# Moving V through TensorE 512 columns at a time, in four column groups and register-addressed loops, in a one-token attention-and-MLP kernel

## The chip, the cores and the metric

One core of one Trainium2 chip. The metric is device time in microseconds (us). The spans of the profile are 1.4 to 1.9 us shorter than the time of the same run, because they run from the first to the last instruction of the program. Executions of the kernel before agree within 0.3%.

## The reference, cut to what matters

One token, two branches, and a scalar gate that mixes them. Branch A is grouped-query attention over the last 4096 positions of a cache, with 32 query heads and 16 key/value heads of size 128. Branch B is an MLP with GELU.

```python
W = min(4096, max(256, Sk // 4))                     # 4096
q = (x @ wq)                                          # 576 -> 32 heads x 128
k = repeat(k_cache[:, :, Sk - W:, :], 2);  v = the same of v_cache
p = softmax(q k^T * Dh**-0.5);  o = p v
a = o.reshape(4096) @ wo                              # 4096 -> 576
b = gelu(x @ w1 + b1) @ w2 + b2                       # 576 -> 4608 -> 576
return g * a + (1 - g) * b                            # g = sigmoid(sum(x * gate_w))
```

All inputs are bf16. The kernel must read K and V (16.8 MB each) and four weight matrices: 53.6 MB in all, for very little arithmetic.

## The kernel before

All large loads are issued in one queue, in program order: w1, wq, eight pieces of K, half of w2, V in groups of four heads (groups 0 to 2 as one load each, group 3 as two halves), wo in two halves, and the rest of w2 in three pieces. The buffers are shared. Their tags are A to D, and a load waits until the last reader of its buffer has finished. V group 3 goes into the buffer of V group 0 (tag C), and wo into that of V group 1 (tag D).

In the V stage each 128x128 block of V is the stationary operand, and 8 columns of probabilities move through it. That is 512 pairs of a weight load and a tiny matmul.

```python
p_t = kt_pool.tile([P, NCK, 8, HB], BF16, name="p_t", tag="kt")
pt = kt_pool.tile([P, NCK, Hq], BF16, name="pt", tag="kt")
# ... exp into p_t, transpose into pt ...
o_ps = ps_m.tile([P, Hq, 1], FP32, name="o_ps", tag="m")
for g in range(NG):                                   # NG = 4 groups of 4 heads
    v_t = big.tile([P, NCK, Dh], BF16, name="v_t", tag="CDAC"[g])
    src = ...
    for u in range(2 if g == NG - 1 else 1):
        n = NCK // 2 if g == NG - 1 else NCK
        nc.sync.dma_start(out=v_t[:, u * n : (u + 1) * n, :]..., in_=src[...])
    for c in range(NCK):                              # NCK = 128
        nc.tensor.matmul(o_ps[:, 8 * g : 8 * g + 8, 0], lhsT=v_t[:, c, :],
                         rhs=pt[:, c, 8 * g : 8 * g + 8],
                         start=(c == 0), stop=(c == NCK - 1))
wo_t = big.tile([P, RO, D], BF16, name="wo_t", tag="D")
# ... load wo in two halves, the rest of w2 in three pieces ...
# ... om = o_ps * (gate / softmax sum), ov = its heads regrouped ...
for r in range(RO):                                   # 32 rows of wo, two matmuls each
    y_add(ov[:, r : r + 1], wo_t[:, r, :])
for f in range(NJ, NF):                               # second half of w2
    y_add(gt[:, f : f + 1], w2_t[:, f, :], stop=(f == NF - 1))
# ... output row, store ...
```

## Time and profile before

| | before |
|---|---|
| time | 134.61 us (134.55 to 134.67, 2 runs) |
| span of the profile | 133.3 us |
| bytes moved | 53.78 MB, mean 403 GB/s |

The profile page cuts the span into 40 slices of 3.33 us each. A digit is the busy share in tenths, and PEclk is the clock granted to TensorE in tenths.

```profile
PE   0239995066499769769779450008923951445881
PEclk9999999999999999999999995555555555558679
DMA  5999989899999999999999999999999999999950
```

The DMA row is 9 from the second slice almost to the end. TensorE (PE) has idle slices, and its clock stands at half in the last third, yet nothing follows from that: the kernel is one uninterrupted stream of loads. The timeline of PE in the last third shows the same. Its columns are start, length, then engine, line and operation; in brackets is the idle time before, and what ended it.

```profile
90.98 6.04 PE L387 MATMUL o_ps<-pt,v_t 128*128 128x8 bf16 x220
99.66 1.10 PE L387 MATMUL o_ps<-pt,v_t 128*128 128x8 bf16 x36 [2.65 <-issue]
102.98 3.71 PE L387 MATMUL o_ps<-pt,v_t 128*128 128x8 bf16 x128 [2.22 <-DMA v_t<-in_A_v_cache_dram]
107.88 1.87 PE L387 MATMUL o_ps<-pt,v_t 128*128 128x8 bf16 x64 [1.19 <-DMA v_t<-in_A_v_cache_dram]
112.79 1.87 PE L387 MATMUL o_ps<-pt,v_t 128*128 128x8 bf16 x64 [3.04 <-DMA v_t<-in_A_v_cache_dram]
118.29 3.52 PE L178 MATMUL y_ps<-wo_t,ov 128*1 128x288 bf16 x32 [3.04 <-DMA wo_t<-in_A_wo_dram]
129.40 1.14 PE L178 MATMUL y_ps<-w_t,gt 128*1 128x288 bf16 x16 [0.40 <-DMA w_t<-in_B_w_dram]
```

A V group of 128 pairs takes 3.7 us (103.0 to 106.7). From the third group on, PE then waits for the next landing. The 64 matmuls with wo run while later loads are in flight, so only the last 16 with w2 are exposed at the end. The DMA issues in the same timeline show how early the queue is refilled. Each line is the first issue of a line of the kernel, and its length runs to the last issue.

```profile
62.22 33.56 SPq L382 DMA_DIRECT2D v_t<-in_A_v_cache_dram  x5
100.79 0.81 SPq L400 DMA_DIRECT2D wo_t<-in_A_wo_dram  x2
101.66 1.37 SPq L402 DMA_DIRECT2D w_t<-in_B_w_dram  x3
```

The last load is issued near 103 us and lands near 130 us, so at that point 27 us of transfers are queued. So the V stage should be able to run somewhat slower at no cost, as long as buffers come free in time to keep that queue filled.

### The profile page before, as it was taken

The numbers are of one execution on the slowest core, as the hardware profiler recorded it, in microseconds if no ns is written. First come the engines' busy times: TensorE is split into PE (matmuls) and PEld (weight loads), VectorE is DVE, ScalarE is ACT, GpSimd is POOL, SyncE is SP. The second block draws the span as 40 slices with busy tenths as digits, with TensorE's granted clock in tenths as the row PEclk, the third lists the DMA queues.
The fourth block names the chain that finished last, engine by engine and source line by source line (L and its number), as shares of the span: only waits on it lengthen the run. The fifth ranks groups of instructions, "written<-read, shape, count | busy, mean of one in ns | idle before, by whom it ended". The sixth has DMA issues, their size and how long they took to land.

```text
span 133.3 us, 2458 instructions
## 1 busy us (share of the span) xinstructions
PE 78.1 (59%) x1126; PEld 51.4 (39%) x1126; DVE 55.2 (41%) x80; ACT 13.0 (10%) x25; POOL 0.7 (1%) x6
## 2 busy tenths in 40 slices
PE   0239995066499769769779450008923951445881
PEld 0118995065134323223233230008913951423540
DVE  6177002202988988988984710663000000100001
ACT  3000000003000000000000059930000000000001
POOL 2000000000000000000000000000000000000000
PEclk9999999999999999999999995555555555558679
DMA  5999989899999999999999999999999999999950
GB/s 155 400 461 436 488 359 487 360 428 428 428 418 428 438 413 420 428 433 428 455 417 441 457 413 403 452 462 403 413 438 403 413 433 427 436 420 399 414 205 0
DMA packets 3190, 53.78 MB, mean 403 GB/s; under 512 B 358, under 2 KB 362, under 8 KB 620
## 3 DMA queue, kind: packets, MB, share of 16 engines
q1 hardware_dynamic: 3170, 53.61, 95.0%
q8 instruction: 9, 0.15, 0.4%
q10 hardware_dynamic: 10, 0.01, 0.0%
q14 instruction: 1, 0.01, 0.0%
HBM read 53.62 MB, written 0.00 MB: 402 GB/s over the span
## 4 chain that ended last, share of the span: by engine, by line
DMA 66%; PE 12%; DVE 8%; ACT 7%; issue 3%; SPq 2%; DVEq 0%
DMA k_t<-in_A_k_cache_dram 26%; DMA w_t<-in_B_w_dram 20%; DMA wq_t<-in_A_wq_dram 20%; ACT p_t L336 7%; PE o_ps L387 5%; DVE kt L285 3%; PE q_ps L242 3%; DVE pt L344 2%; DVE m L306 2%; PE s_ps L294 1%; PE y_ps L178 1%; SPq L77 1%; SPq L400 1%; PE t_ps L362 0%; DVE out_row L422 0%
## 5 line engine op out<-in xcount | busy, mean ns | idle before, releaser
L285 DVE STREAM_TRANSPOSE kt<-k_t 128x2048 f32<-128x2048 f32 x16 | 36.0, 2290 | 11.4 <-DMA k_t<-in_A_k_cache_dram 11.4
L294 PE MATMUL s_ps<-kt,qz_flat 128*128 128x512 bf16 x128 | 31.9, 396 | 9.3 <-DVE kt L285 9.3
L294 PEld LDWEIGHTS <-qz_flat 128*128 128x128 bf16 x128 | 12.8, 100 | 28.1 <-issue 14.3
L387 PE MATMUL o_ps<-pt,v_t 128*128 128x8 bf16 x512 | 14.6, 168 | 9.1 <-DMA v_t<-in_A_v_cache_dram 6.5
L387 PEld LDWEIGHTS <-v_t 128*128 128x128 bf16 x512 | 14.3, 105 | 9.5 <-DMA v_t<-in_A_v_cache_dram 6.7
L336 ACT ACTIVATE p_t<-s_ps,negm 128x512 bf16<-128x512 f32 x8 | 9.7, 1411 | 44.7 <-DVE negm L327 44.7
L204 PE MATMUL h_ps<-x,w_t 128*128 128x2 bf16 x162 | 10.2, 202 | 0.0
L204 PEld LDWEIGHTS <-w_t 128*128 128x128 bf16 x162 | 10.1, 163 | 0.0
L178 PE MATMUL y_ps<-wo_t,ov 128*1 128x288 bf16 x64 | 6.8, 393 | 5.0 <-DMA wo_t<-in_A_wo_dram 5.0
L405 DVE TENSOR_TENSOR om<-o_ps,rgh 128x128 bf16<-128x128 f32 x1 | 0.3, 292 | 22.8 <-PE o_ps L387 22.8
L344 DVE STREAM_TRANSPOSE pt<-p_t 128x2048 bf16<-128x2048 bf16 x2 | 4.6, 2311 | 7.4 <-ACT p_t L336 7.4
L362 PE MATMUL t_ps<-ls,ones 128*128 128x32 f32 x2 | 0.6, 396 | 11.9 <-DVE ls L360 11.9
L242 PE MATMUL q_ps<-x,wq_t 128*128 128x2 bf16 x144 | 4.0, 166 | 5.9 <-DMA wq_t<-in_A_wq_dram 5.9
L422 DVE CAST out_row<-y_ps 1x288 bf16<-1x288 f32 x1 | 0.4, 445 | 15.1 <-PE y_ps L178 15.1
L178 PEld LDWEIGHTS <-ov 128*1 128x1 bf16 x64 | 3.7, 110 | 7.7 <-issue 4.9
L178 PE MATMUL y_ps<-w_t,gt 128*1 128x288 bf16 x72 | 5.9, 298 | 0.6 <-DMA w_t<-in_B_w_dram 0.6
L242 PEld LDWEIGHTS <-wq_t 128*128 128x128 bf16 x144 | 3.9, 104 | 6.0 <-DMA wq_t<-in_A_wq_dram 6.0
L362 PEld LDWEIGHTS t_ps<-ls,ones 128*128 128x128 f32 x2 | 0.5, 310 | 12.2 <-issue 12.2
L421 ACT CAST out_row<-y_ps 1x288 bf16<-1x288 f32 x1 | 0.4, 390 | 42.9 <-PE y_ps L178 42.9
L178 PEld LDWEIGHTS <-gt 128*1 128x1 bf16 x72 | 3.4, 86 | 2.8 <-issue 1.5
L213 DVE COPY hacc<-h_ps 128x36 f32<-128x36 f32 x1 | 0.2, 196 | 9.4 <-PE h_ps L204 9.4
L306 DVE TENSOR_REDUCE m<-s_ps 128x2 f32<-128x2048 f32 x1 | 2.3, 2290 | 2.0 <-PE s_ps L294 2.0
(68 smaller groups left out, 26.9 us busy)
## 6 DMA issues: line engine op xcount, KB each, us to landing
k_t<-in_A_k_cache_dram SPq DMA_DIRECT2D x8, 2048.0 KB, 32.0
v_t<-in_A_v_cache_dram SPq DMA_DIRECT2D x3, 4096.0 KB, 29.8
wq_t<-in_A_wq_dram SPq DMA_DIRECT2D x1, 4608.0 KB, 26.1
wo_t<-in_A_wo_dram SPq DMA_DIRECT2D x2, 2304.0 KB, 20.0
v_t<-in_A_v_cache_dram SPq DMA_DIRECT2D x2, 2048.0 KB
w_t<-in_B_w_dram SPq DMA_DIRECT2D x1, 2880.0 KB, 14.7
w_t<-in_B_w_dram SPq DMA_DIRECT2D x1, 2592.0 KB, 11.3
w_t<-in_B_w_dram SPq DMA_DIRECT2D x1, 2304.0 KB, 8.3
```

The lines of the kernel that those rows point to most:

```text
L77: nc.sync.dma_start(out=w1_t[:, i0:i1, :], in_=w1_src[:, i0:i1, :])
L178: nc.tensor.matmul(y_out[s], lhsT=vec, rhs=row[:, s * DH : (s + 1) * DH], start=start, stop=stop, skip_group_check=True,)
L204: nc.tensor.matmul(h_ps[:, j:NF:NJ], lhsT=w1_t[:, i, j:FH:NJ], rhs=x2[:, i, :], start=False, stop=(i == NI - 1 and j == NJ - 1), skip_grou ...
L242: nc.tensor.matmul(q_ps[:, j : Hq : Hq // 2], lhsT=wq_t[:, i, j * Dh : (j + 1) * Dh], rhs=x2[:, i, :], start=(i == 0 and j == 0), stop=(i ...
L285: nc.vector.transpose(out=kt[:, u * half : (u + 1) * half].bitcast(FP32), in_=k_t[:, f, u * SL // 2 : (u + 1) * SL // 2, :] .rearrange("p ...
L294: nc.tensor.matmul(s_ps[:, u * 512 : (u + 1) * 512].rearrange("p (c k) -> p c k", k=32), lhsT=qz[:, h0 // 2, j, :], rhs=kv[:, u * SL // 4 ...
L306: nc.vector.reduce_max(out=m2[:], in_=s_ps[:].rearrange("p (n b) -> p b n", b=2), axis=AX.X)
L336: nc.scalar.activation(out=p_t[:, cs, :, b], in_=s_ps[:].rearrange("p (c k u b) -> p u b c k", k=8, u=2, b=2)[:, f, b % 2], func=ACT.Exp, ...
L344: nc.vector.transpose(out=pt[:, cs, :].rearrange("p c h -> p (c h)"), in_=p_t[:, cs, :, :].rearrange("p c k b -> p (c k b)"),)
L362: nc.tensor.matmul(t_ps[:], lhsT=ones[:], rhs=ls[:], start=True, stop=True)
L387: nc.tensor.matmul(o_ps[:, 8 * g : 8 * g + 8, 0], lhsT=v_t[:, c, :], rhs=pt[:, c, 8 * g : 8 * g + 8], start=(c == 0), stop=(c == NCK - 1),)
L400: nc.sync.dma_start(out=wo_t[:, r0:r1, :], in_=wo_src[:, r0:r1, :])
```

## The change

The intent is to issue fewer PE instructions. V becomes the moving operand, 512 columns (four blocks) at a time. The stationary operand is 32 columns of probabilities (4 blocks x 8 heads), loaded into one of four column groups of the array. Of each 32 x 512 product only the four diagonal blocks are wanted, so VectorE (DVE) masks and adds them, and an fp32 matmul with a selector sums the rest. The 128 matmuls stand in loops on PE with register addresses (the place of each operand is computed by PE's sequencer, the part of PE that issues its instructions, from the loop counter). Each loop is inside a critical section of the scheduler: a stretch that waits at its entry as a whole. The diff, cut:

```diff
+def grouped_matmul(nc, out, lhsT, rhs, col):
+    pe = nc.tensor
+    return pe.add_instruction(
+        mybir.InstMatmult(
+            start_tensor_calc=False, stop_tensor_calc=False,
+            tile_size=(128, 32), tile_position=(0, 32 * col), ...
-    pt = kt_pool.tile([P, NCK, Hq], BF16, name="pt", tag="kt")
+    pt = kt_pool.tile([P, NG, NCK, 8], BF16, name="pt", tag="kt")
...
+    # m4: four masks; zb: zeros; o4: four PSUM banks, zeroed by four matmuls
+    o_part = const.tile([P, NG, Dh], FP32, name="o_part")
...
-        for c in range(NCK):
-            nc.tensor.matmul(o_ps[:, 8 * g : 8 * g + 8, 0], lhsT=v_t[:, c, :], ...)
+            with tc.tile_critical():
+                with nc.tensor.Fori(u * n // 16, (u + 1) * n // 16) as it:
+                    for j in range(4):
+                        grouped_matmul(
+                            nc,
+                            o4[32 * j : 32 * j + 32, g, :, :].rearrange("p c d -> p (c d)"),
+                            pt[:, g, :, :].rearrange("p c h -> p (c h)")[
+                                :, bass.ds((it * 16 + 4 * j) * 8, 32)
+                            ],
+                            vf[:, bass.ds((it * 16 + 4 * j) * Dh, 4 * Dh)],
+                            j,
+                        )
+        nc.vector.tensor_scalar(out=o_part[:, g, :], in0=o4[:, g, 0, :], scalar1=m4[:, 0:1], ...)
+        for c in range(1, 4):
+            nc.vector.scalar_tensor_tensor(out=o_part[:, g, :], in0=o4[:, g, c, :], ...)
+        nc.tensor.matmul(o_ps[:, 8 * g : 8 * g + 8, 0], lhsT=o_part[:, g, :], rhs=lo8[:], start=True, stop=True)
```

What the diff does not show is what the scheduler makes of the critical sections. I read this from the order of instructions, and the semaphores they wait for, in the built program:

| loop | may start when (besides its own V) | what waits for its end |
|---|---|---|
| V0 | V1 has landed | load of V3, first half |
| V1 | V2 has landed | load of wo, first half |
| V2 | V3, first half, has landed | |
| V3, first half (3a) | wo, first half, has landed | load of V3, second half, and behind it wo's second half and the rest of w2 |
| V3, second half (3b) | wo, second half, has landed | the output |

More of the change, by code (lines that the diff above doesn't have):

```diff
@@ L13 @@
 AX = mybir.AxisListType
+def grouped_matmul(nc, out, lhsT, rhs, col):
+    pe = nc.tensor
+    return pe.add_instruction(
+        mybir.InstMatmult(
+            start_tensor_calc=False,
+            stop_tensor_calc=False,
+            tile_size=(128, 32),
+            tile_position=(0, 32 * col),
+            bass_skip_group_check=True,
+            name=nc.get_next_instruction_name(),
+            engine=mybir.EngineType.PE,
+            ins=[pe.lower_ap(rhs), pe.lower_ap(lhsT, for_matmul_weights=True)],
+            outs=[pe.lower_ap(out)],
+        )
+    )
 @with_exitstack
@@ L344 @@
         nc.vector.transpose(
-            out=pt[:, cs, :].rearrange("p c h -> p (c h)"),
-            in_=p_t[:, cs, :, :].rearrange("p c k b -> p (c k b)"),
+            out=pt[:, :, cs, :].rearrange("p g c h -> p c g h"),
+            in_=p_t[:, cs, :, :].rearrange("p c (g k) b -> p c g (k b)", g=NG),
         )
@@ L371 @@
     )
+    m4 = const.tile([P, 4], FP32, name="m4")
+    nc.vector.reduce_sum(out=m4[:], in_=lo32[:].rearrange("p (c h) -> p c h", c=4), axis=AX.X)
+    zb = const.tile([P, P], BF16, name="zb")
+    nc.vector.memset(zb[:].bitcast(FP32), 0.0)
     o_ps = ps_m.tile([P, Hq, 1], FP32, name="o_ps", tag="m")
+    o4 = ps_s.tile([P, NG, 4, Dh], FP32, name="o4", tag="s_ps")
+    o_part = const.tile([P, NG, Dh], FP32, name="o_part")
+    for g in range(NG):
+        nc.tensor.matmul(
+            o4[:, g, :, :].rearrange("p c d -> p (c d)"),
+            lhsT=zb[:],
+            rhs=zb[:, 0:1].to_broadcast([P, 4 * Dh]),
+            start=True,
+            stop=False,
+            skip_group_check=True,
+        )
     for g in range(NG):
@@ L379 @@
         )
+        vf = v_t[:].rearrange("p c d -> p (c d)")
         for u in range(2 if g == NG - 1 else 1):
@@ L385 @@
             )
-        for c in range(NCK):
-            nc.tensor.matmul(
-                o_ps[:, 8 * g : 8 * g + 8, 0],
-                lhsT=v_t[:, c, :],
-                rhs=pt[:, c, 8 * g : 8 * g + 8],
-                start=(c == 0),
-                stop=(c == NCK - 1),
-            )
+            with tc.tile_critical():
[9 more added lines that the diff above has]
+                            j,
+                        )
+        nc.vector.tensor_scalar(
+            out=o_part[:, g, :], in0=o4[:, g, 0, :], scalar1=m4[:, 0:1], scalar2=None, op0=ALU.mult
+        )
+        for c in range(1, 4):
+            nc.vector.scalar_tensor_tensor(
+                out=o_part[:, g, :],
+                in0=o4[:, g, c, :],
+                scalar=m4[:, c : c + 1],
+                in1=o_part[:, g, :],
+                op0=ALU.mult,
+                op1=ALU.add,
+            )
+        nc.tensor.matmul(
+            o_ps[:, 8 * g : 8 * g + 8, 0], lhsT=o_part[:, g, :], rhs=lo8[:], start=True, stop=True
+        )
     RO = Hq * Dh // P
```

## The prediction

> **What bounds the kernel.** DMA. The slices of the profile show the DMA engines at 0.99 or more in nearly every slice but the first and last, and the queues moved 53.8 MB at 403 GB/s. In the timeline the PE waits for each V landing: group 2 starts at 103.0 us, the halves of group 3 at 107.9 and 112.8, wo at 118.3 and 123.8, the last w2 at 129.4; the span ends at 133.3. All V matmuls (line groups: 512, 14.6 us busy) run in these shadows: 128 take 3.7 us per group, while a group takes about 9.8 us to land. Making them cheaper can gain nothing directly; what counts is when the PE frees buffers, and the order of the loads.
>
> **What the change does.** 512 weight-load/matmul pairs become 128 matmuls (32 columns of weights, 512 moving), in five register-addressed loops, each a critical section. Added: four zeroing matmuls, 16 DVE operations on 128x128 fp32 (0.29 us is what such a one takes in the profile: about 1.2 us per group), four fp32 selector matmuls (0.6 us, as t_ps).
>
> In the built program I read three new orderings:
> 1. Each loop's entry waits for every DMA queued ahead of it, not just its own V: group 0 for V1, group 1 for V2, group 2 for the first half of V3, that half for the first half of wo, the second half of V3 for the second half of wo.
> 2. The second half of V3 is loaded only after the loop over the first half has ended, since a register address counts as reading the whole tile; it now stands behind the first half of wo.
> 3. wo's second half and the rest of w2 are issued only after that.
>
> **Loop time.** The Trainium skill, "TensorE: Matmul & The Clock Gate", Part 3, gives 2.38x for three column tiles, so the four should overlap; one 128x512 takes 0.38 us busy here when warm. But each matmul has a fused address calculation plus one more register operation ahead of it, and the page "Advanced Engine Details and Errata", Control Flow Timing, gives about 108 ns for a compare-and-branch. No trace here shows either. My estimate is 0.9 us per loop turn of four matmuls, sequencer-bound, so 7.5 us per group against 3.7 before (0.45 to 1.5 us are possible).
>
> **Timeline (estimate, from the landings above[...]).** Loop 0: 93.5-101. Loop 1: 103.2-110.7; only then wo's first half is issued: DMA idles from 107.8 to about 112.7; it lands at 118.2. Loop 2: 112.5-120; its combination; half loop 3a to 125.5. Only then V3b: DMA idles from 118.2 to about 127.5. V3b lands 132.5, wo's second half 138, w2 144. Loop 3b starts at 138, ends 142; combination, selector, om, ov about 3 us; then 64 wo matmuls and the w2 ones, which were hidden before, about 9.5 us exposed: 154.5; output 2.7 us: 157. The measured time exceeds the span by 1.3 us: 158.5 us, slower by 18%. Each microsecond of group loop time is worth about 3 us.
>
> **What would show it right.** DMA slices near zero twice after 107 us; the second V3 load issued after wo's first; PE waits at loop entries ended by wo landings; about 10 us of PE work after the last w2 landing; loop turns near 0.9 us.
>
> **What would make it wrong.** Loop turns near 0.45 us (overlap, cheap address work): about 147. Column groups not overlapping[...]: 170 or more. If the waits at loop entries turn out to be satisfied early, the loss shrinks to a few us. A gain over 2% would need the DMA stream itself to get shorter, which nothing here does.
>
> Predicted 158.5 us, range 147 to 172; faster 0.01, within 2% 0.03, slower 0.96.

## The result

| | before | after |
|---|---|---|
| time | 134.61 us | 177.97 us (177.43 to 178.51, 2 runs) |
| ratio | 1 | 1.320, interval 1.312 to 1.328 |
| span | 133.3 us | 176.7 us |
| bytes moved | 53.78 MB | 53.71 MB |

A ratio here is the mean time of one kernel's fast runs over that of the other's of the same rounds, so it is not quite the ratio of the medians quoted. The direction was right and so was its cause, but the loss is 43 us instead of 24, and the time is above the 147 to 172 us that I had named.

The slices of the page after the change are 4.4 us each.

```profile
PE   0179917399977787850147856973883910065893
PEclk9999999999999999985555898798799555558579
DMA  6999989999999999999999609207500049994000
```

The first 22 slices of the DMA row look as before. Then the stream breaks three times. Asked for windows, the trace shows next to no traffic from 101.9 to 106.3 us, from 112.1 to 120.3 us, and from 126.9 to 143.7 us: 29 us in all. At about 162 us the stream is over, and 12 us of PE work and the output follow without any load; before, the output followed almost at once. The same 53.7 MB are moved; the time is in the holes and in the tail, 41 of the 43 us.

The DMA issues and the longest waits of the queue that issues them are shown next. The second view's columns are who waited for whom, total us, times, longest us.

```profile
119.31 0.33 SPq L452 DMA_DIRECT2D wo_t<-in_A_wo_dram  x1
142.38 0.54 SPq L415 DMA_DIRECT2D v_t<-in_A_v_cache_dram  x1
142.97 0.58 SPq L452 DMA_DIRECT2D wo_t<-in_A_wo_dram  x1
143.60 1.72 SPq L454 DMA_DIRECT2D w_t<-in_B_w_dram  x3
```

```profile
SPq L415 <- PEq L419: 44.7, 2, 22.7
SPq L452 <- PEq L419: 13.8, 1, 13.8
```

Before, everything had been issued by 103 us. Now wo's first half goes out at 119.3, and the second half of V3 at 142.4 with all the rest behind it. All three waits (22.7 and 22.0 us at L415, 13.8 us at L452) are for PE's sequencer at L419, the end of a loop. The groups of the page that are new:

```profile
L18 PE MATMUL o<-v_t,pt 128*32 x128 | 40.0, 483 | 24.1 <-DMA wo_t<-in_A_wo_dram 14.1
L443 PE MATMUL o_ps<-lo,o_part 128*128 128x8 f32 x8 | 1.7, 289 | 7.1 <-DVE o_part L435 7.1
L435 DVE SCALAR_TENSOR_TENSOR o_part<-o,m,o_part 128x128 f32<-128x128 f32 x12 | 4.2, 351 | 0.4
```

V's matmuls are now 128 instead of 512, and keep PE busy for 40.0 us instead of 14.6. Each loop, cut from the trace in windows. The columns are from:to, length, busy us and count of PE, of its weight loads and of DVE, granted clock, DMA share, GB/s:

```profile
93.80:104.90 11.10, 9.64 (x32) 3.08 (x32) 0.00 (x0) 0.78 0.58 251
108.00:119.20 11.20, 9.95 (x32) 3.03 (x32) 0.00 (x0) 0.85 0.33 140
122.30:133.50 11.20, 9.67 (x32) 3.04 (x32) 0.00 (x0) 0.85 0.36 155
136.50:142.30 5.80, 5.54 (x16) 1.61 (x16) 0.00 (x0) 0.50 0.00 0
156.30:161.90 5.60, 5.15 (x16) 1.58 (x16) 0.00 (x0) 0.66 0.84 351
```

A group of 32 matmuls takes 11.1 us (the first 10.8) instead of 3.7, and a half group half of that. The half loop at clock 0.50 is no slower than the loop at 0.85: both take 1.42 us per turn. Where the array sets the pace, in experiment 8, a group follows its clock (8.64 us at 0.82, 7.08 us at 1.00). The timeline of the weight loads shows one whole turn of the loop, from 113.71 to 115.15:

```profile
113.71 0.09 PEld L18 LDWEIGHTS o<-v_t,pt 128*32 x1 [0.56 <-issue]
113.97 0.09 PEld L18 LDWEIGHTS o<-v_t,pt 128*32 x1 [0.17 <-issue]
114.22 0.09 PEld L18 LDWEIGHTS o<-v_t,pt 128*32 x1 [0.16 <-issue]
114.47 0.09 PEld L18 LDWEIGHTS o<-v_t,pt 128*32 x1 [0.16 <-issue]
115.15 0.09 PEld L18 LDWEIGHTS o<-v_t,pt 128*32 x1 [0.58 <-issue]
```

The four matmuls follow each other at 0.25 us; then 0.68 us pass until the next turn's first. Every gap is put down to "issue", that is, to nothing that the profile shows as a wait. The sequencer's own instructions (count, then ns min/median/max) show what fills them:

```profile
L18 PEldq FUSED_REGOPS  x200: 42/51/79, 93.8 to 161.3; - x100
L18 PEldq ALU_OP  x24: 32/32/39, 94.1 to 104.3; - x24
L420 PEldq FUSED_REGOPS  x32: 78/78/83, 93.7 to 160.3; - x32
L420 PEldq COMPARE_BRANCH  x32: 76/212/227, 94.8 to 161.5; - x32
```

Ahead of each matmul stand two address instructions (mostly fused ones, FUSED_REGOPS), and each turn ends with a branch of 0.21 us. The branch of the last turn, which falls through, takes 0.08 us.

### The profile page after: what moved, and what is told of

Read it like the earlier page. It is cut to its first block, busy times and chain, and to the rows that moved or that the text cites. A ratio compares the mean times of both kernels' runs of the same rounds, so it can differ in the third digit from the quotient of the medians.

```text
span 176.7 us, 2118 instructions
## 1 busy us (share of the span) xinstructions
PE 107.5 (61%) x754; PEld 51.6 (29%) x754; DVE 61.0 (35%) x98; ACT 13.0 (7%) x25; POOL 0.7 (0%) x6
## 2 busy tenths in 40 slices
DMA packets 3186, 53.71 MB, mean 304 GB/s; under 512 B 358, under 2 KB 362, under 8 KB 620
## 5 line engine op out<-in xcount | busy, mean ns | idle before, releaser
L18 PE MATMUL o<-v_t,pt 128*32 x128 | 40.0, 483 | 24.1 <-DMA wo_t<-in_A_wo_dram 14.1
L302 DVE STREAM_TRANSPOSE kt<-k_t 128x2048 f32<-128x2048 f32 x16 | 36.0, 2290 | 10.6 <-DMA k_t<-in_A_k_cache_dram 10.6
L311 PE MATMUL s_ps<-kt,qz_flat 128*128 128x512 bf16 x128 | 32.6, 403 | 8.7 <-DVE kt L302 8.5
L18 PEld LDWEIGHTS o<-v_t,pt 128*32 x128 | 12.3, 96 | 50.9 <-issue 48.2
L431 DVE TENSOR_SCALAR o_part<-o,m 128x128 f32<-128x128 f32 x4 | 1.4, 350 | 65.5 <-PEq L419 65.5
L399 PE MATMUL o<-zb 128*128 128x512 bf16 x4 | 1.9, 622 | 8.7 <-ACT p_t L353 8.7
L443 PE MATMUL o_ps<-lo,o_part 128*128 128x8 f32 x8 | 1.7, 289 | 7.1 <-DVE o_part L435 7.1
L435 DVE SCALAR_TENSOR_TENSOR o_part<-o,m,o_part 128x128 f32<-128x128 f32 x12 | 4.2, 351 | 0.4
L443 PEld LDWEIGHTS o_ps<-lo,o_part 128*128 128x128 f32 x8 | 1.4, 218 | 8.3 <-DVE o_part L435 6.2
## 6 DMA issues: line engine op xcount, KB each, us to landing
wo_t<-in_A_wo_dram SPq DMA_DIRECT2D x2, 2304.0 KB, 12.5
w_t<-in_B_w_dram SPq DMA_DIRECT2D x1, 2880.0 KB, 14.6
```

The source lines that it names most:

```text
L18: return pe.add_instruction(mybir.InstMatmult(start_tensor_calc=False, stop_tensor_calc=False, tile_size=(128, 32), tile_position=(0, 32 * ...
L302: nc.vector.transpose(out=kt[:, u * half : (u + 1) * half].bitcast(FP32), in_=k_t[:, f, u * SL // 2 : (u + 1) * SL // 2, :] .rearrange("p ...
L311: nc.tensor.matmul(s_ps[:, u * 512 : (u + 1) * 512].rearrange("p (c k) -> p c k", k=32), lhsT=qz[:, h0 // 2, j, :], rhs=kv[:, u * SL // 4 ...
L399: nc.tensor.matmul(o4[:, g, :, :].rearrange("p c d -> p (c d)"), lhsT=zb[:], rhs=zb[:, 0:1].to_broadcast([P, 4 * Dh]), start=True, stop=False,
L431: nc.vector.tensor_scalar(out=o_part[:, g, :], in0=o4[:, g, 0, :], scalar1=m4[:, 0:1], scalar2=None, op0=ALU.mult)
L435: nc.vector.scalar_tensor_tensor(out=o_part[:, g, :], in0=o4[:, g, c, :], scalar=m4[:, c : c + 1], in1=o_part[:, g, :], op0=ALU.mult, op1= ...
```

## The experiments

**Theory.** (1) PE's sequencer, not the array, sets the loop turn of 1.4 us. (2) The critical sections change which load waits for which loop, so a longer loop starves the DMA queue, and the second half of V3 starves it once more. (3) Nothing else in the change costs anything. **Rivals:** the column groups don't really overlap, so the array sets the turn; the masks, selectors and the new probability layout cost time; the order alone is the loss, or the loop alone.

All eight kernels gave correct results. Ratios are to the kernel before on the same chip in the same rounds: 134.68 us for experiments 1, 2, 3 and 5, 134.82 us for the others. The change itself was measured beside a kernel before of 134.61 us, so differences between these groups are good to a few tenths of a microsecond. With one core, a run counts as slow when it is over 1.5% above the fastest of its kernel.

### 1. The same matmuls without loop and without critical section

```diff
-            with tc.tile_critical():
-                with nc.tensor.Fori(u * n // 16, (u + 1) * n // 16) as it:
-                    for j in range(4):
+            for it in range(u * n // 16, (u + 1) * n // 16):
+                for j in range(4):
                     grouped_matmul(...)      # bass.ds(x, 32) -> x : x + 32, and so on
```

> The same four column groups, zeroing, masks and selectors, but the 128 matmuls written out with fixed addresses and ordinary tile dependencies: no loop, no critical section. Theory (register-addressed loops and the order that the critical sections force are the whole loss): the loads go back to their order of before and stay fed, the added 3 us from the last V matmul to the output vector hide behind the landing of wo: 134 to 136 us. Rival (the strided probability layout, the fp32 masks and selectors or the column groups themselves cost time): 140 us or more.

Measured: 134.97 us, ratio 1.001 (0.9996 to 1.0029). It is the same as before the change. The windows of its first three V groups (here without the column of weight loads), and its issues:

```profile
91.20:94.90 3.70, 3.55 (x32) 0.01 (x1) 0.53 0.99 425
96.80:99.30 2.50, 2.46 (x32) 0.00 (x0) 0.75 1.01 433
102.40:106.10 3.70, 3.60 (x32) 0.03 (x1) 0.50 1.01 425
```

```profile
94.88 1.18 SPq L415 DMA_DIRECT2D v_t<-in_A_v_cache_dram  x2
99.33 0.81 SPq L451 DMA_DIRECT2D wo_t<-in_A_wo_dram  x2
```

The order of loads is back, the queue is fed early, and the DMA share is about 1. Part (3) of the theory holds: column groups, masks, selectors and layout cost nothing here; what they take lies behind the landings that PE waits for. The intended gain is also visible: there is hardly any. A group takes 2.5 to 3.6 us, against 3.7 us for 128 pairs of the old form at a clock of 0.5.

### 2. Fixed addresses, critical sections kept

```diff
             with tc.tile_critical():
-                with nc.tensor.Fori(u * n // 16, (u + 1) * n // 16) as it:
+                for it in range(u * n // 16, (u + 1) * n // 16):
                     for j in range(4):       # fixed addresses
```

> The 128 matmuls written out with fixed addresses but each group inside a critical section as in the change, so that entry waits and order of loads are those of the change and only the loop is gone. Theory (overlapping groups, about 3.4 us per V group at the low clock): the time model of the prediction with 3.4 us gives 149 us (146 to 152), with the DMA still idle once before the second half of V3. If the order alone were the whole loss: about 175 us. If the loop's length alone were: 135 us.

Measured: 150.51 us, ratio 1.117 (1.111 to 1.123), within the expectation. The second half of V3 is issued at 117.9 us, instead of 142.4 with loops and 95.2 before:

```profile
97.54 0.54 SPq L415 DMA_DIRECT2D v_t<-in_A_v_cache_dram  x1
107.23 0.33 SPq L452 DMA_DIRECT2D wo_t<-in_A_wo_dram  x1
117.89 0.54 SPq L415 DMA_DIRECT2D v_t<-in_A_v_cache_dram  x1
118.48 0.58 SPq L452 DMA_DIRECT2D wo_t<-in_A_wo_dram  x1
```

PE's half loop 3a, just before that issue:

```profile
115.81 1.90 PE L18 MATMUL o<-v_t,pt 128*32 128x512 bf16 x16 [0.95 <-DMA wo_t<-in_A_wo_dram]
```

So the critical sections by themselves cost 15.5 us (150.5 less 135.0), and the loops inside them another 27.5 us (178.0 less 150.5). The critical sections alone are not the whole loss; the loops alone were not run.

These lines also correct a reason in the prediction. The second half of V3 waits for the end of half loop 3a (117.7 us) though no address is in a register here, and in experiment 1 it doesn't wait. So the critical section is enough to cause that wait; "a register address counts as reading the whole tile" is not needed for it.

### 3. Loops and critical sections, V3 in one load

```diff
-        for u in range(2 if g == NG - 1 else 1):
-            n = NCK // 2 if g == NG - 1 else NCK
+        for u in range(1):
+            n = NCK
```

> Loops and critical sections as in the change, but V3 is one load and one loop of 8 turns, so no load waits for half a loop. Theory: loops stay 11.2 us each with 3.1 us between; loop 3 ends near 148 us of the span instead of 162, all loads have landed by then; 164 us in all (161 to 167). Rival (the stall before the second half of V3 is not what counts, the loops are in any case the chain): 174 us or more.

Measured: 163.91 us, ratio 1.217 (1.213 to 1.221), as the theory had it. No load waits for half of V3 any more: wo and w2 are all issued by 122 us, and w2 has landed when the last loop ends at 148 us. Its DMA slices, 4.04 us each, are empty from the 36th (141.5 us) on:

```profile
DMA  6999999999999999999999997079928999200000
```

What remains is four loops in a row on PE. Splitting V3 in two, which the kernel before does with a full stream, costs 14 us here (178.0 less 163.9).

### 4. Fixed addresses in critical sections, V3 in one load

The edits of 2 and 3 together.

> Fixed addresses inside critical sections, and V3 as one load, so no load waits for half of V3 to be consumed; the entry waits are all still there. Theory: the entry waits alone cost little once the loop is short: 137.5 us (136 to 140). Rival (the entry waits themselves are the main part of the 16 us that fixed addresses in critical sections lost): 145 us or more.

Measured: 139.91 us (138.54 to 140.11), ratio 1.038 (1.037 to 1.040). This is at the upper edge of the expectation, 2.4 us above its centre, and far from the rival. The stream never breaks (this kernel's DMA slices):

```profile
DMA  5999998999999999999999999999999999999400
```

The last V group starts at 119.5 us, 3 us after the one before it has ended: one combination, one selector and one entry lie between them. After it come all 100 matmuls with wo and w2, from 126.0 to 134.0 us, while the loads are over by 130 us: PE, and no longer the stream, ends last. In experiment 1 most of these matmuls run between the landings. So of the 15.5 us of experiment 2, about 4.9 us (139.9 less 135.0) are the entry waits, together with V3 landing as a whole, and 10.6 us (150.5 less 139.9) the wait of V3's second half.

### 5. Eight matmuls per turn

```diff
-                with nc.tensor.Fori(u * n // 16, (u + 1) * n // 16) as it:
-                    for j in range(4):
+                with nc.tensor.Fori(u * n // 32, (u + 1) * n // 32) as it:
+                    for j in range(8):       # group j % 4
```

> Eight matmuls per loop turn and half the turns. Theory (the sequencer sets the turn: 0.255 us for each matmul with its address work and 0.395 us for each turn): 2.43 us a turn, 9.7 us per group instead of 11.3, and about 4 times the difference in the end: 171.5 us (169.5 to 173.5). Rival (the array sets the pace, or the cost grows with the number of instructions alone): group loops stay at 11 us or more, 177 us or more.

Measured: 169.7 us in the one fast run; the other three, 172.3 to 173.3 us, count as slow against it. All four are within the expectation and below the rival's 177. The profiled run is one of the slow ones (172.33 us, clock 0.84), and I read from it only the loops, whose turn did not follow the clock above. They take 9.4 to 9.6 us from the first matmul to the end of the last, against 10.8 to 11.1 in the change. The saving of about 1.5 us per group is what half the turn ends are worth; matmuls still follow each other at 0.25 us. Why one run was 3 us faster stays open; it had the highest clock of the four (0.877), but no trace of it was kept.

### 6. One address register per turn

```diff
-                            pt[:, g, :, :]...[:, bass.ds((it * 16 + 4 * j) * 8, 32)],
-                            vf[:, bass.ds((it * 16 + 4 * j) * Dh, 4 * Dh)],
+                            pt[:, g, :, :].rearrange("p (t c) h -> p t (c h)", c=16)[
+                                :, bass.ds(it, 1), 32 * j : 32 * j + 32]...,
+                            vf.rearrange("p (t x) -> p t x", x=16 * Dh)[
+                                :, bass.ds(it, 1), 4 * j * Dh : (4 * j + 4) * Dh]...,
```

> The loops of the change, with addresses written as one dynamic index per turn and fixed slices within it: one fused address operation fewer before three of four matmuls. Theory (sequencer): a turn of about 1.1 us instead of 1.415, groups near 8.9 us, and four times the difference at the end: 168 us (165 to 171). Rival (the turn is bound by branch or array): 176 us or more.

Measured: 167.56 us, ratio 1.244 (1.241 to 1.246). The theory said 168. Not one matmul, wait or load was changed, only the address arithmetic. The windows of its first two loops:

```profile
93.90:102.60 8.70, 7.51 (x32) 3.06 (x32) 0.00 (x0) 0.81 0.74 320
105.80:114.50 8.70, 7.51 (x32) 3.06 (x32) 0.00 (x0) 0.80 0.42 181
```

Loops of 8.6 us instead of 11.1, 2.5 us less, bring 10.4 us in the whole. The factor is about four because all four groups (three loops and two half loops) stand in a row and each counts in full: in the two profiled runs the last loop ends 9.7 us earlier, at 152.1 instead of 161.7. The other 1.2 us between these two runs are in the tail, where the 64 matmuls with wo took 5.8 us at a granted clock of 0.71, against 6.7 us at 0.60 in the change. The trace shows 120 fused address operations at L18 here, against 200 in the change.

### 7. Loops, all matmuls in one column group

```diff
-                            o4[32 * j : 32 * j + 32, g, :, :]...,
+                            o4[0:32, g, :, :]...,          # and tile_position (0, 0)
```

> The change's loops, but all four matmuls of a turn go to column group 0, so they can't overlap in the array. Theory (the sequencer spaces matmuls by 0.255 us, and a 512-column matmul streams in 0.21 us at full clock): little changes, loops of about 11.3 to 12.5 us, 181 us (178 to 184). Rival (the loop's time is array time that the groups share): loops several times as long, over 200 us.

Measured: 175.7 and 177.6 us in the two fast runs (two more, 178.8 and 179.3 us, count as slow), against 178.0 for the change. That is just below what I expected and far from the rival. Without any overlap in the array the full loops are as long as with it:

```profile
108.10:119.30 11.20, 10.53 (x32) 3.59 (x32) 0.00 (x0) 0.76 0.33 140
122.40:133.60 11.20, 10.08 (x32) 3.29 (x32) 0.00 (x0) 0.85 0.36 155
```

The column groups, which were the point of the change, do nothing in these loops. The last half loop alone is longer with one group, 6.0 us against 5.4; the clock was low there (0.59 and 0.66).

### 8. No loop, no critical section, one column group

The edit of experiment 1, and with it:

```diff
-                        o4[32 * j : 32 * j + 32, g, :, :]..., ..., j)
+                        o4[0:32, g, :, :]..., ..., 0)
```

> Fixed addresses, no critical sections, but one column group: 32 matmuls of 512 columns in a row per V group. Theory: without the loop the array sets the pace, 0.43 us each at the low clock and 0.21 at the full one, so 7 to 10 us per group where four groups took 2.5 to 3.6 us; V then runs just behind the loads and is exposed at the end: 145 us (140 to 151). Rival (four groups overlap only in the modelled ends of the matmuls): 135 to 136 us as with four groups.

Measured: 140.80 us, ratio 1.045 (1.043 to 1.047).

```profile
91.40:100.10 8.70, 8.64 (x32) 0.01 (x1) 0.82 0.98 422
102.00:109.20 7.20, 7.08 (x32) 0.04 (x1) 1.00 0.94 385
```

Here the array sets the pace: 7.1 us for 32 matmuls at full clock, or 0.22 us each, against 2.5 to 3.6 us with four groups at a lower clock. So the groups do overlap, and their overlap is not a matter of modelled ends. Counted in time x clock, an estimate from these windows, four groups work 3.8 to 3.9 times as fast as one (7.08 x 1.00 over 2.46 x 0.75 and 3.60 x 0.50). The time is at the lower end of what I expected; from the second group on the granted clock was 1.00, so the groups took 7 us and not up to 10.

### Summary

| loop | critical sections | V3 | column groups | us |
|---|---|---|---|---|
| before the change | | two loads | | 134.7 |
| none | no | two loads | 4 | 135.0 |
| none | no | two loads | 1 | 140.8 |
| none | yes | one load | 4 | 139.9 |
| none | yes | two loads | 4 | 150.5 |
| yes | yes | one load | 4 | 163.9 |
| yes, one address register per turn | yes | two loads | 4 | 167.6 |
| yes, eight matmuls per turn | yes | two loads | 4 | 169.7 (one fast run) |
| yes (the change) | yes | two loads | 4 | 178.0 |
| yes | yes | two loads | 1 | 175.7, 177.6 (two fast runs) |

No version points below the kernel before, since it already moves its bytes without a hole. I ran none for that. A loop without a critical section was not tried, so its entry waits were taken away only together with the loop.

## Why the prediction was right or wrong

**What bounds the kernel: right.** Experiment 1 removes three quarters of V's matmuls and ends at the same time.

**The three new orderings: right, one for a wrong reason.** All three are in the trace; the reason given for the second, the register address, is not needed (experiment 2). V3's second half is issued at 142.4 us, behind wo's first half, and only after half loop 3a. The last half loop waits for wo: 14.1 us of idle before it.

```profile
156.32 4.05 PE L18 MATMUL o<-v_t,pt 128*32 x12 [14.11 <-DMA wo_t<-in_A_wo_dram]
164.96 6.68 PE L195 MATMUL y_ps<-wo_t,ov 128*1 128x288 bf16 x64 [0.28 <-DVE ov L465]
```

One detail of it was moot: the entry waits of loops 1, 2 and 3a had long been satisfied, because PE was later than the loads. Only loop 3b certainly waited at its entry for a landing; before loop 0 PE was idle for 2.7 us, which the trace of the change puts down to "issue" and that of experiment 2 to V's landing. The first hole, 101.9 to 106.3 us, was not forecast: with loop 0 ending at 101 us instead of 104.7, the next load would have been queued at about the time the stream ran dry.

**The exposed tail: right.** From the end of the last loop to the end of the span I had 15 us (142 to 157). The trace has 15.0 (161.7 to 176.7). Its length moves with the granted clock: 13.8 us in experiment 6.

**"My estimate is 0.9 us per loop turn of four matmuls, sequencer-bound, so 7.5 us per group": this is the term that was mis-sized.** "Sequencer-bound" was right (experiments 5, 6 and 7). The turn is 1.4 us instead of 0.9, and the group 11.1 us instead of 7.5. I had counted "a fused address calculation plus one more register operation" and then given them too little: with the two of them a matmul follows the last after 0.25 us, and 0.68 us pass from the last of a turn to the first of the next. The Trainium skill, "Advanced Engine Details and Errata", Control Flow Timing, gives about 108 ns for a compare-and-branch; the trace has 212 ns in the median and 76 for one that falls through. The same skill's "TensorE: Matmul & The Clock Gate", Part 3, was no misleading source: it gives 2.38x for three column tiles, and experiments 1 and 8 show four of them at 2.0 to 2.9 times the speed of one (7.08 us over 3.60 and 2.46), with the one at full clock and the four at 0.50 and 0.75.

**"Each microsecond of group loop time is worth about 3 us": wrong once the loops are longer than about 6 us.** Up to there loop 1 starts at the landing of V2 (103.4 us in experiment 2), so loop 0, which starts at 93.9 us and is followed by 3.2 us of other work, has slack. Beyond it all four groups stand in a row on PE, and each counts in full. Experiment 6 shows the factor: the last loop ends 9.7 us earlier for 2.5 us per loop. Against the timeline of the prediction the loops and half loops together are about 14 us longer (44.0 us instead of 30.2); that is most of the 19.5 us by which the time exceeded it (178.0 less 158.5).

**The time between loops: about 4 us of the rest.** I allowed 5.8 us for the three gaps between loops 0, 1, 2 and 3a. The trace has 3.2 to 3.3 us for each (104.7 to 108.0 for the first): DVE's four operations, 0.35 us each rather than my 0.29, then the selector, then a row of semaphore waits and a branch at the entry, 1.0 to 1.1 us of PE idle between the selector and the first V matmul, put down to "issue". The Trainium skill, "TensorEngine Tiling (Array Packing)", PSUM Bottleneck, warns that tiling speeds up TensorE but not the evacuation of PSUM. Here the evacuation (1.4 us on DVE) and what follows it are as long as a whole group of matmuls without the loop (2.5 to 3.6 us). Another 1.6 us are in the wait from the end of half loop 3a to the landing of wo's second half, 14.1 us where I had 12.5.

**The range: too narrow on the slow side.** I named 1.5 us per turn as possible, but with the factor of three it led only to 172.

## What to carry to other kernels

When loads bound a kernel, a change to a compute stage is worth what it does to the moment at which each load can be issued, so read the built program's waits before counting engine time. A loop with register addresses has a price per matmul and per turn on the sequencer, and faster array work inside it is wasted as long as that price is higher. A critical section can order loads and compute anew, and so put what stands in it on the path that decides the time: here one microsecond more per loop cost four, because all four groups stood in a row.

## What the Trainium skill lacked or had wrong

- "Advanced Engine Details and Errata", Control Flow Timing: compare-and-branch about 108 ns. On PE the runs show 212 ns for a taken one (median of 32, of which 27 are taken) and 76 ns for one that falls through, and 0.68 us from a turn's last matmul to the next turn's first.
- No page gives the cost of register addresses on PE: fused address operations of 42 to 79 ns each and, with two such operations ahead, 0.25 us per matmul whatever the array's clock; 0.15 us with one (experiment 6).
- "TensorE: Matmul & The Clock Gate", Part 3, has three column tiles at most among its column-only figures. Four took 3.6 us for 32 matmuls of 512 columns at clock 0.50 and 2.5 us at 0.75, against 7.1 us for one group at 1.00.
- "TensorEngine Tiling (Array Packing)", Performance Considerations, does not say that packing is lost where address work on the sequencer feeds the array slower than one tile works: four groups 178.0 us, one group 175.7 and 177.6 us.
